# Keeping a recurrent state once for two heads and copying it out with GpSimd

## The chip, the cores and the metric

The kernel runs on one core of one Trainium2 chip. The metric is the device time of one execution in microseconds. A core has five engines that run side by side: TensorE (PE, matrix multiply, with its weight loads as PEld), VectorE (DVE), ScalarE (ACT), GpSimd (POOL) and SyncE (SP, here a queue of DMAs). They wait for each other through semaphores.

## The reference

Two blocks follow each other. The first is a gated linear recurrence for 4 batches of 8 heads, 768 tokens, head size 48: a 48 x 48 state a head is decayed row by row and given an outer product at each token, and a query reads it.

```python
f = 1.0 / (1.0 + np.exp(-f_logit))
for t in range(S):
    state = f[:, :, t, :, None] * state + einsum('bhd,bhe->bhde', k[:, :, t], v[:, :, t])
    y[:, :, t] = einsum('bhd,bhde->bhe', q[:, :, t], state)
```

The result is laid out as x, 3072 tokens by 384. The second block computes h = x @ w_in (384 to 2048), g = h * erf(softplus(h)), and g @ w_out (2048 to 384). Everything is float32.

## The kernel before, in words

The tokens are cut into 24 chunks g of 128 (six a batch), two chunks to a block of 256 tokens, and each chunk into two half chunks c of 64. Half chunks are numbered k = 2g + c. The eight heads are four pairs a; the head r of a pair lives on partitions 64r to 64r + 47. Each chunk passes these stages:

- `stage_d` (L381): a matmul with a triangle sums the logs of the decays (ps_d, L387), ACT takes exponentials (dp L390, kd L393), SP copies the decay totals of a chunk into `Tall` by DMA (L398, from chunk 3 on), VectorE makes the scaled q and k (qd L402, kd L406).
- `stage_t` (L410): TensorE transposes them (ps_t, L418); ACT or VectorE copies them out (qA L425, kT L427 or L429). Before that it runs a `late` state step of the chunk before, if there is one.
- `stage_s` (L450): TensorE computes the state increments dS (L467) and the scores (L475) into one PSUM tile `sc`; the scores are masked into qA, by VectorE (L503) or, in chunks 3 to 9, by ACT copies (L495) and GpSimd (L498). Then `next_state(2g)` runs at once and `next_state(2g + 1)` is put in `late`.
- `stage_y` (L511): 64 small matmuls (L532) read qA and `sv`; ACT copies the result to xT (L536).

`sv` is the operand buffer of L532, two of them in turn (`svs`). It holds for each head r and half chunk c the state on the partitions of that head, and the v rows on the other half of the partitions (loaded by DMA at L254, or by ACT at L251 in the first three chunks). y(g) reads the states that k = 2g - 1 and k = 2g left.

`next_state` (L433) works directly on `sv`: for each of the two heads it adds the increment from PSUM to the state in the old place and writes the new place (L445), and multiplies there by the totals (L446). The first half chunk of a batch has one multiply (L443), and GpSimd sets the state of that batch to zero (L455).

The second block hides in between: `hidden` (L594, evacuated by ACT at L601), `activate` (exp and tanh on ACT, L157, L160, L566; products on VectorE, L165, L568), `project_first` (L684) and `project` (L735, with sums by L622 and L743). In the first part of the run the weights are loaded as raw 64-bit words, and `round_piece` makes float32 of them: one ACT and six VectorE instructions a piece (L311 to L336), 16 pieces.

The order of all work is written out by hand: `slots` gives the sequence of TensorE's matmuls of an iteration, and the lists `at` and `todo` say at which slot a stage is called. Each engine takes its instructions in that order, and the framework adds the semaphore waits that data and buffers ask for. The `sc` tile comes from a pool with one buffer, and is taken anew in each `stage_s`.

Of the kernel before, what the change touches and what calls it, by code (L numbers as in the profile page):

```python
# [43 lines left out]
FP32 = mybir.dt.float32  # L44
# [30 lines left out]
def kernel(  # L75
# [33 lines left out]
    def fixed(name, shape, dtype=FP32, pool=const):  # L109
        return pool.tile(shape, dtype, name=name)  # L110
# [67 lines left out]
    ps_at = main.enter_context(tc.tile_pool(name="ps_at", bufs=2, space=PSUM))  # L178
    ps_moe = main.enter_context(tc.tile_pool(name="ps_moe", bufs=2, space=PSUM))

    NV, NQ, NG = 3, 3, 12
    ADJACENT = 5
    vts = [fixed(f"vt{i}", [P, d_model], pool=fix) for i in range(NV)]
# [6 lines left out]
    kds = [fixed(f"kd{i}", [P, H, DP], pool=fix) for i in range(2)]  # L190
    dps = [fixed(f"dp{i}", [P, H, DP], pool=fix) for i in range(2)]
    Tall = fixed("Tall", [P, n_chunks, 2, HP], pool=fix)
    Hring = fixed("Hg", [P, NG * FG * TB], pool=fix)

    DH = d_model // 2
# [237 lines left out]
    def next_state(k, dS):  # L433

        g, c = divmod(k, 2)
        g1, c1 = divmod(k + 1, 2)
        for r in range(2):
            old = svs[g % NSV][rows(r), r, c, :, PAD : PAD + D]
            new = svs[g1 % NSV][rows(r), r, c1, :, PAD : PAD + D]
            total = Tall[rows(r), g, c, :].unsqueeze(2).broadcast_to((D, HP, D))  # L440
            add = dS[rows(r), c, :].rearrange("p (a d) -> p a d", a=HP)
            if k % (2 * NCH) == 0:
                nc.vector.tensor_tensor(out=new, in0=add, in1=total, op=ALU.mult)  # L443
                continue
            nc.vector.tensor_tensor(out=new, in0=add, in1=old, op=ALU.add)  # L445
            nc.vector.tensor_tensor(  # L446
                out=new, in0=new, in1=total, op=ALU.mult
            )

    def stage_s(g):  # L450
        b, n = divmod(g, NCH)
        last = n == NCH - 1
        if n == 0:
            for r in range(2):
                nc.gpsimd.memset(svs[g % NSV][rows(r), r, 0, :, PAD : PAD + D], 0.0)  # L455
        qA, kT = qAs[g], kTs.pop(g)
        ps = ps_sc.tile([P, 2, 512], FP32, name="sc", tag="sc")

        sc = ps[:, :, 0 : HP * C].rearrange("s r (a t) -> s r a t", t=C)
        dS = ps[:, :, HP * C : HP * (C + D)]  # L460
        totals = ps[:, 0, HP * (C + D) : HP * (C + D) + 2 * HP]
        vt, kd = vts[g % NV], kds[g % 2]
        for a in range(HP):
            for c in range(1 if last else 2):
                for r in range(2):
                    h = 2 * a + r
                    nc.tensor.matmul(  # L467
                        dS[rows(r), c, D * a : D * (a + 1)],
                        lhsT=kd[half(c), h, 0:D], rhs=vt[half(c), D * h : D * (h + 1)],
                        start=True, stop=True,  # L470
                    )
        for a in range(HP):
            for r in range(2):
                for c in range(2):
                    nc.tensor.matmul(  # L475
                        sc[half(c), r, a, :], lhsT=kT[rows(r), a, half(c)],
                        rhs=qA[rows(r), r, a, half(c)], start=True, stop=True,
                    )
        if g < FIRST:

            pairs = dps[g % 2][:].rearrange("t (a r) d -> t a (r d)", r=2)
            for a in range(HP):
                nc.tensor.matmul(
                    totals[:, 2 * a : 2 * a + 2], lhsT=pairs[:, a, :], rhs=ident[:, C - 1 : P : C],
                    start=True, stop=True,
                )
            nc.vector.tensor_copy(
                out=Tall[:, g].rearrange("p c a -> p a c"),
                in_=totals.rearrange("p (a c) -> p a c", c=2),
            )  # L490
        for c in range(2):
            for r in range(2):
                if FIRST <= g < 2 * ADJACENT:

                    nc.scalar.copy(out=qA[half(1 - r), r, :, half(c)], in_=sc[half(c), r])  # L495
                    if c == 1:
                        flat = qA[half(1 - r), r].rearrange("s a (c t) -> s (a c) t", c=2)
                        nc.gpsimd.affine_select(  # L498
                            out=flat, in_=flat, pattern=[[0, 2 * HP], [1, C]], compare_op=ALU.is_ge,
                            fill=0.0, base=0, channel_multiplier=-1,  # L500
                        )
                    continue
                nc.vector.tensor_tensor(  # L503
                    out=qA[half(1 - r), r, :, half(c)], in0=sc[half(c), r],
                    in1=tri1[half(c)].unsqueeze(1).broadcast_to((C, HP, C)), op=ALU.mult,
                )
        next_state(2 * g, dS)
        if not last:
            late[g] = lambda: next_state(2 * g + 1, dS)
# [191 lines left out]
    def project(blk):  # L701


        ops = [ps_moe.tile([P, 2, 512], FP32, name="ops", tag="moe") for _ in range(2)]
        end = blk == n_blocks - 1
        ops.append(ps_sc.tile([P, 2, 512], FP32, name="ops", tag="sc") if end else ops[1])
        place = {n: ops[i][:, j, k * DH : (k + 1) * DH] for n, (i, j, k) in {
            1: (0, 0, 0), 2: (0, 1, 0), 6: (0, 1, 1), 5: (1, 0, 0), 7: (1, 0, 1), 3: (2, 1, 0), 4: (2, 1, 1),
        }.items()}
        first = [1, 2, 5, 3]  # L710
        if end:
            place[4] = ps_at.tile([P, 512], FP32, name="ops4", tag="at")[:, 0:DH]
            first.append(4)

        def pair(n):
            i, j = {2: (0, 1), 5: (1, 0), 3: (2, 1)}[n]
            return ops[i][:, j, 0 : 2 * DH].rearrange("p (n c) -> p n c", n=2)

        def products(gis, ns):
            for gi in gis:  # L720
                gr = groups[blk, gi]
                while gr["sums"] is None:
                    sum_step()
                a11, a12, a21, a22 = blocks(gr["h"])
                w = w_out_sb[:, FG * gi : FG * (gi + 1), :]
                s, t = gr["sums"], w_sums(gi)
                for j in range(2):
                    w1, w2 = w[:, j, :], w[:, 2 + j, :]
                    for n in ns:
                        x, y = {  # L730
                            1: (a11, w1[:, 0:DH]), 2: (a12, w2[:, 0:DH]), 3: (s[2], w2[:, DH:]),
                            4: (a22, t[:, 3, j, :]), 5: (s[0], t[:, 0, j, :]),
                            6: (s[1], t[:, 1, j, :]), 7: (a21, t[:, 2, j, :]),
                        }[n]
                        nc.tensor.matmul(  # L735
                            place[n], lhsT=x[:, j, :], rhs=y,
                            start=(gi == 0 and j == 0 and n in first),
                            stop=(gi == n_g - 1 and j == 1), skip_group_check=True,
                        )
                        yield  # L740

        def plus(out, x, y):
            nc.vector.tensor_tensor(out=out, in0=x, in1=y, op=ALU.add)  # L743

        o = rows_sb
        yield from products((0, 1), (1, 2, 6))
        yield from products((0,), (5, 7, 3, 4))
        to_sum.appendleft(sum_h(groups[blk, 3]))
        yield from products((1,), (5, 7, 3, 4))
        yield from products((2, 3), (1, 2, 6))  # L750
        nc.scalar.copy(out=o[:, 3, :], in_=place[1])  # L751

        plus(o[:, 0:5:4, :], o[:, 3:4, :].broadcast_to((P, 2, DH)), pair(2))
        def fives():

            plus(o[:, 3:5, :], o[:, 4:5, :].broadcast_to((P, 2, DH)), pair(5))

        yield from products((2, 3), (5, 7))
        if end:

            fives()
            yield from products((2, 3), (3,))
            plus(o[:, 1, :], o[:, 3, :], place[3])
            store_tile(blk, 0, nc.sync)
            plus(o[:, 3, :], o[:, 3, :], place[7])
            yield from products((2, 3), (4,))
            plus(o[:, 2, :], o[:, 4, :], place[4])
            store_tile(blk, 1, nc.scalar)
            return
        yield from products((2, 3), (3, 4))  # L770
        fives()
        plus(o[:, 1:3, :], o[:, 3:5, :], pair(3))
        plus(o[:, 3, :], o[:, 3, :], place[7])
        store(blk)
# [42 lines left out]
    with tc.manual_schedule():  # L817
# [62 lines left out]
        def weights_steps(n):  # L880
            for _ in range(n):
                weights_step()

        busy.append(ps_moe.tile([P, 2, 512], FP32, name="busy", tag="moe")[:, 0, 0:P])
        keep_busy(10)
        prepare(0, 0, 1)
# [340 lines left out]
```

## Time and profile before

| | |
|---|---|
| timed runs, median (3 runs) | 618.53 us (618.06 to 619.01) |
| span of the profiled execution | 616.6 us |
| that execution's own time beyond its span | not recorded; the median lies 1.9 us above the span |
| TensorE busy | 588.3 us (95%) |
| VectorE busy | 459.7 us (75%), 785 instructions |
| ACT busy | 382.9 us (62%) |
| GpSimd busy | 14.9 us (2%), 33 instructions |
| state instructions L443, L445, L446 | 8, 80 and 80, of 355, 354 and 358 ns |
| DMA engines, 0 to 16 us and 16 to 40 us | 98% and 96% busy |

The page gives each engine's busy time, rows of instructions grouped by line, and the chain of work that ended last: from the last instruction back, at each step to what released it. A row gives busy us, mean ns of one, and after the second bar the idle time of the engine just before, with what ended it. A timeline row gives start and length in us from the span's start. Time in which an engine idles but which lies beside a busy bottleneck costs nothing.

### The profile page before, as it was taken

How to read it: one execution, taken by the hardware profiler on the slowest of the kernel's cores; microseconds unless marked ns; L12 is line 12 of the kernel's file. 1: busy time of each engine (PE TensorE's matmuls, PEld its weight loads, DVE VectorE, ACT ScalarE, POOL GpSimd, SP SyncE). 2: the span in 40 equal slices, each digit the busy share in tenths (PEclk: the TensorE clock that was granted, in tenths of full speed). 3: DMA queues.
4: the chain of work that ended last, by engine and by line, in shares of the span. 5: the costliest groups of instructions: out<-in, count | busy, mean ns of one | idle time of the engine just before them, and what ended most of it. 6: DMA issues, size and time to landing. Idle time of an engine off the chain costs nothing.

```text
span 616.6 us, 13769 instructions
## 1 busy us (share of the span) xinstructions
PE 588.3 (95%) x5729; PEld 514.5 (83%) x5729; DVE 459.7 (75%) x785; ACT 382.9 (62%) x483; POOL 14.9 (2%) x33
## 2 busy tenths in 40 slices
PE   8778799999999999999999999999999999999996
PEld 7556688887655689989989988988988989989996
DVE  4898998697489597896896875896886795656651
ACT  5735365987875678875866585875775666366000
POOL 1000011010000000000000000000000000000000
PEclk9987899999999999999999999999999999999999
DMA  9998753441241222133133132042130000000000
GB/s 201 248 228 208 199 175 63 71 88 17 53 77 28 41 63 52 25 81 54 33 71 53 32 73 53 14 91 53 15 65 15 3 27 0 28 1 0 27 27 30
DMA packets 155604, 41.36 MB, mean 67 GB/s; under 512 B 147344, under 2 KB 150416, under 8 KB 155536
## 3 DMA queue, kind: packets, MB, share of 16 engines
q1 hardware_dynamic: 153312, 39.82, 29.6%
q8 instruction: 47, 0.77, 0.5%
q10 hardware_dynamic: 2224, 0.59, 0.4%
q14 instruction: 21, 0.17, 0.1%
HBM read 35.59 MB, written 4.72 MB: 65 GB/s over the span
## 4 chain that ended last, share of the span: by engine, by line
PE 74%; DVE 11%; ACT 8%; DMA 3%; issue 2%; SPq 1%; POOL 0%; DVEq 0%; ACTq 0%; POOLq 0%
PE hps L594 31%; PE ops L735 25%; PE ops L684 7%; PE y L532 3%; PE ps_t L418 3%; PE ps_d L387 2%; ACT x L160 2%; PE sc L467 1%; PE sc L475 1%; DVE sv L445 1%; DVE sv L446 1%; DVE w_in_sb L322 1%; DVE Hg L568 1%; DVE w_in_sb L336 1%; PE busy L379 1%
## 5 line engine op out<-in xcount | busy, mean ns | idle before, releaser
L594 PE MATMUL hps<-xT,w_in_sb 128*128 128x256 f32 x1152 | 264.7, 386 | 5.0 <-DVE w_in_sb L336 2.9
L594 PEld LDWEIGHTS hps<-xT,w_in_sb 128*128 128x128 f32 x1152 | 218.5, 193 | 39.2 <-ACT xT L536 2.8
L165 DVE SCALAR_TENSOR_TENSOR e<-x,e 128x1024 f32<-128x1024 f32 x96 | 117.1, 1220 | 13.2 <-ACT x L160 12.6
L160 ACT ACTIVATE x<-Hg,serf_bias 128x1024 f32<-128x1024 f32 x88 | 97.5, 1140 | 0.2
L157 ACT ACTIVATE e<-Hg 128x1024 f32<-128x1024 f32 x44 | 46.5, 1058 | 61.7 <-DVE Hg L568 57.6
L735 PE MATMUL ops<-wT,Hg 128*128 128x192 f32 x320 | 78.4, 328 | 0.0
L568 DVE TENSOR_TENSOR Hg<-Hg,e 128x1024 f32<-128x1024 f32 x44 | 53.7, 1222 | 22.6 <-ACT e L566 22.5
L735 PE MATMUL ops<-wT,scratch 128*128 128x192 f32 x288 | 67.8, 326 | 0.9 <-DVE scratch L743 0.9
L735 PE MATMUL ops<-w_out_sb,Hg 128*128 128x192 f32 x320 | 65.1, 326 | 0.0
L601 ACT COPY Hg<-hps 128x1024 f32<-128x1024 f32 x44 | 44.4, 1010 | 32.7 <-PE hps L594 32.4
L735 PEld LDWEIGHTS ops<-wT,Hg 128*128 128x128 f32 x320 | 55.7, 190 | 1.9
L735 PEld LDWEIGHTS ops<-w_out_sb,Hg 128*128 128x128 f32 x320 | 54.6, 190 | 2.0
L566 ACT ACTIVATE e<-e 128x1024 f32<-128x1024 f32 x48 | 50.3, 1048 | 1.9 <-DVE e L165 1.8
L735 PEld LDWEIGHTS ops<-wT,scratch 128*128 128x128 f32 x288 | 50.2, 190 | 1.1 <-issue 1.1
L503 DVE TENSOR_TENSOR qA<-sc,tri 64x256 f32<-64x256 f32 x68 | 28.7, 422 | 27.3 <-PE sc L475 26.3
L743 DVE TENSOR_TENSOR scratch<-scratch,ops 128x384 f32<-128x384 f32 (+1 forms) x41 | 20.3, 494 | 29.5 <-ACT scratch L751 23.0
L532 PEld LDWEIGHTS y<-qA,sv 128*32 128x32 f32 x1536 | 24.9, 113 | 19.6 <-issue 12.4
L532 PE MATMUL y<-qA,sv 128*32 128x64 f32 x1536 | 29.9, 226 | 10.9 <-issue 5.1
L425 ACT COPY qA<-ps_t 64x512 f32<-64x512 f32 x48 | 27.7, 577 | 19.4 <-PE ps_t L418 19.0
L402 DVE TENSOR_TENSOR qd<-qn,dp 128x384 f32<-128x384 f32 x24 | 13.4, 556 | 33.6 <-ACT dp L390 33.5
L735 PE MATMUL ops<-w_out_sb,scratch 128*128 128x192 f32 x144 | 34.7, 326 | 0.0
L445 DVE TENSOR_TENSOR sv<-sc,sv 48x192 f32<-48x192 f32 x80 | 28.3, 354 | 8.3 <-ACT qA L495 6.9
(111 smaller groups left out, 648.1 us busy)
## 6 DMA issues: line engine op xcount, KB each, us to landing
lt<-in_f_logit_dram SPq DMA_DIRECT2D x24, 192.0 KB, 3.7
qn<-in_q_dram SPq DMA_DIRECT2D x24, 192.0 KB, 3.4
kn<-in_k_dram SPq DMA_DIRECT2D x23, 192.0 KB, 3.7
vt<-in_v_dram SPq DMA_DIRECT2D x23, 192.0 KB, 3.7
out_dram<-scratch SPq DMA_DIRECT2D x11, 384.0 KB, 2.6
sv<-in_v_dram SPq DMA_DIRECT2D x84, 48.0 KB, 2.8
w_out_sb<-in_moe_w_in_dram SPq DMA_DIRECT2D x4, 768.0 KB, 6.1
Hg<-in_moe_w_in_dram SPq DMA_DIRECT2D x4, 768.0 KB, 6.6
```

Source lines behind the costliest of these rows:

```text
L157: nc.scalar.activation(out=dst[:], in_=h, func=AF.Exp)
L160: nc.scalar.activation(out=dst[:], in_=h, func=AF.Tanh, bias=serf_bias[:, i : i + 1], scale=SERF_KAB[i][0])
L165: nc.vector.scalar_tensor_tensor(out=e[:], in0=x[:], scalar=SERF_KAB[i][2], in1=e[:], op0=ALU.add, op1=ALU.mult)
L445: nc.vector.tensor_tensor(out=new, in0=add, in1=old, op=ALU.add)
L503: nc.vector.tensor_tensor(out=qA[half(1 - r), r, :, half(c)], in0=sc[half(c), r], in1=tri1[half(c)].unsqueeze(1).broadcast_to((C, HP, C)), ...
L532: nc.tensor.matmul(y[M * i : M * (i + 1), kt, half(c)], lhsT=sv[:, r, c, a, o : o + M], rhs=qA[:, r, a, half(c)], start=(n == 0), stop=Tru ...
L566: nc.scalar.activation(out=e[:], in_=e[:], func=AF.Tanh, scale=SERF_C)
L568: nc.vector.tensor_tensor(out=h, in0=h, in1=e[:], op=ALU.mult)
L594: nc.tensor.matmul(hps[:, j, :], lhsT=w_in_sb[:, kt, ft * P : (ft + 1) * P], rhs=xTs[blk][:, kt, :], start=(kt == 0), stop=(kt == n_k - 1),)
L601: nc.scalar.copy(out=gr["h"], in_=hps[:])
L684: nc.tensor.matmul(ops[:, tt, 0:d_model], lhsT=gr["h"][:, j, tt * P : (tt + 1) * P], rhs=w_out_sb[:, ft, :], start=(ft == 0), stop=(ft == ...
L735: nc.tensor.matmul(place[n], lhsT=x[:, j, :], rhs=y, start=(gi == 0 and j == 0 and n in first), stop=(gi == n_g - 1 and j == 1), skip_grou ...
```

## The change

The state of a pair's two heads is kept once, in a tile `state` of 128 partitions, of which rows 0 to 111 (48 of the one head, 16 unused, 48 of the other) are worked on by single instructions. A half chunk has one add (dS from PSUM plus `state`) and one multiply (by the totals), both in place, and then two GpSimd copies, one a head, from `state` into the new place in `sv`. The unused rows must hold numbers, so the PSUM tile `sc` is taken once for the whole run, and VectorE clears its increment part ahead of the first chunk. The last projection uses that tile where it took one from the pool.

```diff
+    sc_all = ps_sc.tile([P, 2, 512], FP32, name="sc", tag="sc")
...
+    STATE = DP + D
+    state = fixed("state", [P, HP, D], pool=fix)
...
         g, c = divmod(k, 2)
         g1, c1 = divmod(k + 1, 2)
+        total = Tall[0:STATE, g, c, :].unsqueeze(2).broadcast_to((STATE, HP, D))
+        add = dS[0:STATE, c, :].rearrange("p (a d) -> p a d", a=HP)
+        if k % (2 * NCH) == 0:
+            nc.vector.tensor_tensor(out=state[0:STATE], in0=add, in1=total, op=ALU.mult)
+        else:
+            nc.vector.tensor_tensor(out=state[0:STATE], in0=add, in1=state[0:STATE], op=ALU.add)
+            nc.vector.tensor_tensor(out=state[0:STATE], in0=state[0:STATE], in1=total, op=ALU.mult)
         for r in range(2):
-            old = svs[g % NSV][rows(r), r, c, :, PAD : PAD + D]
-            new = svs[g1 % NSV][rows(r), r, c1, :, PAD : PAD + D]
-            total = Tall[rows(r), g, c, :].unsqueeze(2).broadcast_to((D, HP, D))
-            add = dS[rows(r), c, :].rearrange("p (a d) -> p a d", a=HP)
-            if k % (2 * NCH) == 0:
-                nc.vector.tensor_tensor(out=new, in0=add, in1=total, op=ALU.mult)
-                continue
-            nc.vector.tensor_tensor(out=new, in0=add, in1=old, op=ALU.add)
-            nc.vector.tensor_tensor(
-                out=new, in0=new, in1=total, op=ALU.mult
+            nc.gpsimd.tensor_copy(
+                out=svs[g1 % NSV][rows(r), r, c1, :, PAD : PAD + D], in_=state[rows(r)]
             )
...
-        ps = ps_sc.tile([P, 2, 512], FP32, name="sc", tag="sc")
-
+        ps = sc_all
...
-        ops.append(ps_sc.tile([P, 2, 512], FP32, name="ops", tag="sc") if end else ops[1])
+        ops.append(sc_all if end else ops[1])
...
+        nc.vector.memset(sc_all[:, :, HP * C : HP * (C + D)], 0.0)
         busy.append(ps_moe.tile([P, 2, 512], FP32, name="busy", tag="moe")[:, 0, 0:P])
         keep_busy(10)
         prepare(0, 0, 1)
```

## The prediction

> **What bounds the kernel now.** I read the page's first part, then a table of busy time by stretch of the span, then the chain of work that ended last, and last the rows and the timeline of the concerned instructions.
>
> ```profile
> PE 588.3 (95%) x5729; PEld 514.5 (83%) x5729; DVE 459.7 (75%) x785; ACT 382.9 (62%) x483; POOL 14.9 (2%) x33
> ```
>
> TensorE is the bound as an average, but averages hide the stages. The table by stretch (window; then window length, busy us of each engine, granted clock, DMA share, GB/s) shows two:
>
> ```profile
> 16.00:72.00 56.00, 42.02 (x589) 33.45 (x587) 51.11 (x92) 27.28 (x49) 1.31 (x2) 0.88 0.90 235
> 72.00:130.00 58.00, 57.32 (x665) 48.19 (x666) 48.55 (x80) 42.44 (x66) 7.40 (x10) 0.97 0.47 102
> ...
> 220.00:500.00 280.00, 279.00 (x2935) 255.24 (x2934) 221.50 (x382) 195.96 (x228) 0.50 (x2) 1.00 0.24 45
> ```
>
> From 16 to 72 us TensorE is busy for 42.0 of 56 us and VectorE for 51.1. From 220 to 500 TensorE works 279 of 280 us, so no VectorE time saved there can move the end. Only the first stretch can. The chain confirms it (start, length, what):
>
> ```profile
> 24.67 0.36 DVE sv L445
> 25.05 0.35 DVE sv L446
> 25.43 0.37 DVE sv L445
> 25.83 0.36 DVE sv L446
> 26.21 0.97 DVE w_out_sb L331
> ...
> 71.65 0.48 DVE qd L402
> 72.12 0.14 issue
> 72.26 1.88 PE ps_t L418 x8
> ```
>
> From 17.5 us on the chain runs mostly over VectorE, until TensorE at 72.26 has waited 3.16 us for qd (L402) and takes over for good. The four state instructions of each half chunk lie on it, 0.385 us apart (24.67 to 26.21 is four). In this stretch VectorE idles only twice: 0.77 us for ACT at 17.49 (L313) and 1.85 us for ACT at 54.22 (L445).
>
> **What the Trainium skill says.** "SBUF — State Buffer", section "SBUF: two separate sides": VectorE and GpSimd share one port pair as an exclusive lock, held for a whole instruction; a VectorE instruction takes it in a 2-port mode or with two SBUF inputs, and the loser blocks. The trace agrees in part. Here GpSimd's masking of qA (L498) meets VectorE:
>
> ```profile
> 54.60 0.83 DVE L446 TENSOR_TENSOR sv<-sv,Tall 48x192 f32<-48x192 f32 x1
> ...
> 98.16 0.95 DVE L336 TENSOR_TENSOR w_out_sb<-w_out_sb 128x768 f32<-128x768 f32 x1
> ...
> 99.53 0.35 DVE L446 TENSOR_TENSOR sv<-sv,Tall 48x192 f32<-48x192 f32 x1
> 98.27 2.12 POOL L498 TENSOR_SCALAR_AFFINE_SELECT qA<-qA 64x512 f32<-64x512 f32 x2 [14.26 <-issue]
> ```
>
> L446, two SBUF inputs, usually 0.354, took 0.83 while L498 ran. The L498 pair that started during L336 took 2.12, where the undisturbed pair at 53.86 took 1.37: it was blocked some 0.75 us. But L446 at 99.53 also ran beside L498, undisturbed; there the two worked on different partitions (0 to 47 against 64 to 127), at 54.60 on the same. So I take the lock to bite where partitions overlap; nearly all VectorE work here is 128 partitions wide, so it will.
>
> "GPSIMD Engine Reference", section 4.1: an operation with one input runs at about line rate on GpSimd, one with two at half of VectorE's. The change gives GpSimd copies only. "VectorE: DVE Perf Modes", section "Rules for kernel authors": minimize the count of instructions. The trace agrees that partitions are free: 64x256 (L503) takes 422 ns, 128x256 (L622) 420 ns.
>
> **Part by part.** *VectorE instructions.* 44 half chunks: four begin a batch (one instruction a head), 40 have two a head.
>
> ```profile
> L446 DVE TENSOR_TENSOR sv<-sv,Tall 48x192 f32<-48x192 f32 x80 | 28.7, 358 | 2.8
> L445 DVE TENSOR_TENSOR sv<-sc,sv 48x192 f32<-48x192 f32 x80 | 28.3, 354 | 8.3 <-ACT qA L495 6.9
> ...
> L498 POOL TENSOR_SCALAR_AFFINE_SELECT qA<-qA 64x512 f32<-64x512 f32 x14 | 11.2, 803 | 157.6 <-issue 79.5 <-ACT qA L495 77.6
> ...
> L841 POOL COPY tri<-tri 64x64 f32<-64x64 f32 x2 | 0.5, 232 | 0.1
> ```
>
> 168 instructions become 84 of the same free size, so the same 0.355: 84 x 0.355 = 29.8 us off VectorE's 459.7. From 16 to 72 lie half chunks 0 to 7, where 1 + 7 x 2 = 15 go. At 0.385 that is 5.8; half chunk 0's share is worth nothing, as L313 behind it waits for ACT until 17.49 anyway. Left: 7 x 0.77 = 5.4 us. The other 69 go under a full TensorE: nothing. Their cover is TensorE's own work; if it went, each half chunk would be worth the same 0.77.
>
> *GpSimd copies*, 88 of 48x192. Price from both sides: above the 48x192 memset (L455, 0.252), below the 64x512 masking (0.651 to 0.701 undisturbed). Between the 64x64 copy (0.232) and that, by elements: 0.232 + 128 x 0.98 ns = 0.36. I take 0.35; ends 0.25 and 0.65. Two make 31 us on an engine with 14.9 of 616.6.
>
> *What the copies cost VectorE.* Right behind the multiply stands a wide instruction (L402, L331, L359, L313, L326: 0.35 to 0.96) that takes the lock before the multiply's completion reaches GpSimd. So a copy waits for it, then the next VectorE instruction waits for the copy. At 54.60 a 512-element masking cost VectorE 0.48; by elements a 192-element copy costs 0.18, at most its 0.35, at least 0 if the two slip past each other. I take 0.2: 14 copies, 2.8 us.
>
> *New waits.* The next add waits for both copies, since they read `state`. Where the adds stand close (half chunks 2 and 3: 2.0 us from the multiply's end to the next add) this can bind by some 0.3; it is within the 0.2 a copy. Queued behind that add is the whole rounding of weights. y(g) (L532) now waits for GpSimd in place of VectorE. From half chunk 8 on y stands over 3 us behind (state done 100.65, y at 104.07) or far more, and hides it. Earlier there are three tight hand-overs, y(1) at 26.24, y(2) at 38.31 and y(3) at 55.3: old completion was 1.5 us after the first add; new is add and multiply 0.73, a wait of 0 to 0.96, two copies 0.7, a wait between them: 1.5 to 3.2. So y(2) comes no earlier than before, and neither does ps_d(3) behind it; its dp from ACT ends at 41.82 + 0.49 = 42.31. qd (L402) at 43.43 can thus gain at most 1.1, though VectorE would have 5 x 0.77 - 10 x 0.2 = 1.85 by then. Lost: 0.75. At half chunk 6 the multiply covers both heads' partitions and still meets L498, as one of the two old ones did: no change. On GpSimd's queue the copies stand behind L498 of their own chunk, and the next L498 behind copies: it is over 10 us later. Copies wait for the y that last read the buffer, long done. SP's and ACT's queues keep their order.
>
> *PSUM tile kept once.* It removes the exchange of a tile whose readers were done; TensorE is shown to wait 0.2 us for L445 there in all. ACT's copies L495 get a wait for the previous add, done some 10 us before. Nothing.
>
> *Memset of the PSUM tile*, 384 elements, on VectorE ahead of the first clamp (L359, 4.31). 128 elements take 0.165 and 1280 take 1.125: 0.38. Behind it stand clamp, exp, ln (ending 5.74) and ps_d (6.08, behind warm-up matmuls). Some 0.2 is hidden; 0 to 0.4 is paid, I take 0.2.
>
> **Sum.** Until L402 of chunk 3: 1.1. Half chunks 6 and 7: 2 x 0.77 - 4 x 0.2 = 0.7. Memset: -0.2. Together 1.6 us earlier at 72.26, which TensorE can take, since it waits 3.16 there; from then on TensorE's work is the same. The profiled execution has a span of 616.6, and the median of the timed runs, 618.53, lies 1.9 above it. I forecast a span of 615.0 and 618.5 - 1.6 = 616.9. A result within 0.2% (1.24 us) of before can't be told from no change.
>
> **Rivals.**
> *The lock gives it back.* Copies hold VectorE for their full 0.35: 14 x 0.35 = 4.9 of 5.4, and the memset 0.2 against the 0.5 left: 618.2. For it: the skill's whole-instruction lock. Against: 0.48 at 54.60 was less than L498's 0.68.
> *The copies slip through.* The two heads lie on different partitions, and VectorE hardly stalls: then the gain is capped by TensorE's 3.16 us at 72.26: 618.5 - 3.2 + 0.2 = 615.5. For it: 99.53. Against: 54.60 and 98.27.
> *The hand-over to y becomes the bound (slower).* If each copy waits out a full 0.96 instruction, and copies cost nearer 0.65, both end 0.96 + 0.65 + 0.96 + 0.65 = 3.2 us behind the multiply, 1.7 later than a hand-over can bear even with 0.7 gained. Paid at y(2) and y(3), through ps_d and xT, twice 1.7 less 1.5 gained: 620.4. It decides once the second copy ends over about 2 us behind the multiply at y(1) to y(3). For it: L498 was blocked 0.75 once. Against: VectorE itself stays the later of the two at most places.
> *A 112-partition instruction costs more than a 48-partition one.* Against: 422 and 420 above. Then 618.7.
>
> **How the numbers follow.** Forecast 0.42 (own range 615.9 to 617.9), lock gives back 0.25, slips through 0.13, hand-over 0.17, wider instruction 0.03. Forecast counts as faster for about three quarters, slips through wholly: 0.45; hand-over is slower: 0.17; the rest 0.38. The range leaves out the outer part of the hand-over and the best of the slip: 615.0 to 620.0.
>
> **What would show it.** VectorE's busy time near 430 us; state instructions of 0.355 over 112 partitions; copies near 0.35, longer where a wide VectorE instruction started first; VectorE's L331, L336, L313 lengthened by about 0.2 behind them; ps_t of chunk 5 near 70.7 in place of 72.26; TensorE full after it. Wrong, if that ps_t is later than 72, if y(1) to y(3) wait for GpSimd over 1 us, or if time moves after 130 us.

## The result and the profile after

The changed kernel takes 613.04 us (median of 4 runs, 612.16 to 613.8) where the kernel before, run beside it on the same chip, takes 618.5; the ratio is 0.9914, with an interval of 0.99 to 0.9929. That is 5.5 us faster. The forecast was 616.9 with a range of 615.0 to 620.0: the direction was right, the size was not. The span of the profiled execution went from 616.6 to 610.9.

The page of the changed kernel, its busy line and the row of the new copies (two columns after the bar: busy us and mean ns; after the second bar the idle time before):

```profile
PE 588.6 (96%) x5729; PEld 514.6 (84%) x5729; DVE 428.7 (70%) x702; ACT 382.7 (63%) x483; POOL 92.8 (15%) x121
...
L449 POOL COPY sv<-state 48x192 f32<-48x192 f32 x88 | 76.3, 867 | 319.0 <-DVE state L447 222.9
```

VectorE lost 31.0 us, as forecast (29.8). A copy was to take 0.35. Its mean is 0.867, but the trace gives a minimum of 0.334, a median of 0.347 and a maximum of 3.99: the price alone was right, and some copies are held up for long.

The table by stretch, same columns as before:

```profile
16.00:72.00 56.00, 47.51 (x612) 38.30 (x611) 49.62 (x85) 30.36 (x54) 14.40 (x18) 0.85 0.91 238
72.00:130.00 58.00, 57.59 (x730) 48.22 (x729) 46.64 (x71) 43.83 (x68) 18.84 (x24) 1.00 0.47 99
...
220.00:500.00 280.00, 278.24 (x2925) 254.26 (x2924) 204.67 (x339) 193.37 (x225) 37.82 (x46) 1.00 0.23 45
```

From 16 to 72 us TensorE now works for 47.5 us instead of 42.0, on more matmuls (612 for 589) and at a lower granted clock (0.85 for 0.88). From 72 to 130 the granted clock is 1.00 where it was 0.97. And from 220 to 500 TensorE is busy for less than before, 278.2 instead of 279.0: something has begun to hold it there.

The chain of work around 25 us, where four state instructions stood before:

```profile
24.28 0.37 DVE state L446
24.65 0.02 issue
24.67 0.37 DVE state L447
25.04 0.05 issue
25.09 1.01 POOL sv L449
26.10 0.06 issue
26.16 0.97 POOL sv L449
27.13 0.04 issue
27.17 0.67 PE y L534 x28
```

VectorE and GpSimd over the same two microseconds (start, length):

```profile
24.28 0.36 DVE L446 TENSOR_TENSOR state<-sc,state 112x192 f32<-112x192 f32 x1
24.67 0.36 DVE L447 TENSOR_TENSOR state<-state,Tall 112x192 f32<-112x192 f32 x1
24.95 0.95 DVE L335 SCALAR_TENSOR_TENSOR w_out_sb<-w_out_sb 128x768 f32<-128x768 uint32 x1
25.94 0.97 DVE L340 TENSOR_TENSOR w_in_sb<-w_out_sb,w_in_sb 128x768 f32<-128x768 f32 x1
...
25.09 2.03 POOL L449 COPY sv<-state 48x192 f32<-48x192 f32 x2 [4.58 <-DVE state L447]
```

The two copies take 2.03 us instead of 0.7: each ends about 0.2 us after a wide VectorE instruction has ended (25.90, 26.91). L335 and L340 take 0.95 and 0.97, against 0.97 and 0.96 before. So at this place the one that yields is GpSimd, not VectorE. Also, L335 starts 0.28 us after the multiply; before, it started 0.38 after it (25.83 to 26.21). A half chunk thus saves 0.87 and not 0.77.

The late copies are on the chain, though. The second half of y(1) waited 0.71 us for them, and the chain goes on from it through ScalarE and TensorE, which ran at half clock from 27.95 to 38.19, to a wait of VectorE for TensorE's sums:

```profile
27.86 0.49 ACT xT L538
...
28.39 2.07 PE hps L596 x4
30.47 0.82 PE sc L469 x32
31.29 0.88 PE sc L477 x32
32.17 1.81 PE sc L485 x8
```

```profile
34.00 0.17 DVE L489 COPY Tall<-sc 128x8 f32<-128x8 f32 x1 [1.15 <-PE sc L485]
```

GpSimd's masking meets the multiply as it did before (the copies wait behind both):

```profile
52.15 0.77 DVE L447 TENSOR_TENSOR state<-state,Tall 112x192 f32<-112x192 f32 x1
...
51.35 1.37 POOL L500 TENSOR_SCALAR_AFFINE_SELECT qA<-qA 64x512 f32<-64x512 f32 x2 [7.29 <-ACT qA L497]
53.06 1.56 POOL L449 COPY sv<-state 48x192 f32<-48x192 f32 x2 [0.34 <-DVE state L447]
```

TensorE's take-over of the run, the transposes that waited 3.16 us at 72.26. (The prediction calls them chunk 5's. Counted from 0, as everywhere else, they are chunk 4's.)

```profile
68.09 0.63 PE L422 MATMUL ps_t<-ident,qd 128*128 128x128 f32 x4
68.56 0.63 PE L422 MATMUL ps_t<-ident,kd 128*128 128x128 f32 x4
```

They come 4.17 us earlier and wait for nothing. They are also shorter: 0.63 instead of 1.03 and 1.06, because TensorE ran at half clock there before and does not now. The twelve matmuls behind take 2.76 instead of 3.66. Near the end stands the loss. TensorE, then GpSimd and VectorE at the last y (chunk 23):

```profile
486.44 0.65 PE L534 MATMUL y<-qA,sv 128*32 128x64 f32 x32
488.70 1.04 PE L534 MATMUL y<-qA,sv 128*32 128x64 f32 x32 [1.61 <-POOL sv L449]
...
485.19 3.85 POOL L449 COPY sv<-state 48x192 f32<-48x192 f32 x2 [7.01 <-DVE state L447]
...
484.95 1.22 DVE L165 SCALAR_TENSOR_TENSOR e<-x,e 128x1024 f32<-128x1024 f32 x1
486.09 1.22 DVE L570 TENSOR_TENSOR Hg<-Hg,e 128x1024 f32<-128x1024 f32 x1
487.22 1.22 DVE L165 SCALAR_TENSOR_TENSOR e<-x,e 128x1024 f32<-128x1024 f32 x1
```

Behind three VectorE instructions in a row the two copies need 3.85 us, and the second half of y waits for them.

With the same instruction found in both traces, the lead of the changed kernel can be followed (start before, start after, lead):

| place | before | after | lead | what was added |
|---|---|---|---|---|
| transposes of chunk 4 | 72.26 | 68.09 | 4.17 | VectorE's shorter way |
| y(4) | 91.45 | 85.63 | 5.82 | +1.65, full clock behind the take-over |
| y(10) | 208.36 | 201.41 | 6.95 | +1.13, of it 1.04 at y(8) and y(9) |
| transposes of chunk 18 | 365.08 | 357.22 | 7.86 | +0.91, at one wait |
| end of the span | 616.6 | 610.9 | 5.7 | -2.2, the last y |

At y(8) and y(9) TensorE waited 1.37 and 1.51 us, and now 0.91 and 0.93. The profile names GpSimd for it, but its copies had ended at 144.90, and ACT's copy of qA ended at 145.44, 0.1 us ahead of y(8): y waits for ACT, which runs behind VectorE's L570. The one wait before chunk 18 was this line of before, which has no counterpart after:

```profile
361.12 4.12 PE L594 MATMUL hps<-xT,w_in_sb 128*128 128x256 f32 x18 [1.00 <-DVE scratch L743]
```

It is the one missing microsecond in "279 of 280". The table sets one profile beside one; over the profiles of all runs but one the first transposes start between 8.04 and 9.12 us (e7, below, is the exception).

### The profile page after: what moved, and what is told of

It is laid out like the page before. It is cut to its first block, busy times and chain, and to the rows that moved or that the text cites. A ratio compares the mean times of both kernels' runs of the same rounds, so it can differ in the third digit from the quotient of the medians.

```text
span 610.9 us, 13911 instructions
## 1 busy us (share of the span) xinstructions
PE 588.6 (96%) x5729; PEld 514.6 (84%) x5729; DVE 428.7 (70%) x702; ACT 382.7 (63%) x483; POOL 92.8 (15%) x121
## 3 DMA queue, kind: packets, MB, share of 16 engines
q1 hardware_dynamic: 153312, 39.82, 29.8%
## 4 chain that ended last, share of the span: by engine, by line
PE 81%; DVE 7%; ACT 7%; issue 2%; POOL 2%; ACTq 0%; POOLq 0%; DVEq 0%
PE hps L596 37%; PE ops L737 25%; PE ops L686 5%; PE y L534 3%; PE ps_t L422 3%; PE ps_d L391 2%; PE sc L477 2%; PE sc L469 2%; POOL sv L449 2%; ACT x L160 1%; DVE qA L505 1%; DVE Hg L570 1%; ACT e L568 1%; PE busy L383 1%; ACT e L157 1%
## 5 line engine op out<-in xcount | busy, mean ns | idle before, releaser
L449 POOL COPY sv<-state 48x192 f32<-48x192 f32 x88 | 76.3, 867 | 319.0 <-DVE state L447 222.9
L570 DVE TENSOR_TENSOR Hg<-Hg,e 128x1024 f32<-128x1024 f32 x44 | 53.7, 1221 | 24.6 <-ACT e L568 24.5
L737 PE MATMUL ops<-w_out_sb,scratch 128*128 128x192 f32 x132 | 32.2, 326 | 0.0
```

Of the source, the lines that this page charges most:

```text
L449: nc.gpsimd.tensor_copy(out=svs[g1 % NSV][rows(r), r, c1, :, PAD : PAD + D], in_=state[rows(r)])
L570: nc.vector.tensor_tensor(out=h, in0=h, in1=e[:], op=ALU.mult)
L737: nc.tensor.matmul(place[n], lhsT=x[:, j, :], rhs=y, start=(gi == 0 and j == 0 and n in first), stop=(gi == n_g - 1 and j == 1), skip_grou ...
```

## The experiments

Theory: what counts is VectorE's time before the take-over. It passes to TensorE in full, because GpSimd yields at the shared port. On top comes the half clock that no longer follows TensorE's wait, and the last y gives 2.2 us back. Rivals: the single PSUM tile; the steady part, where 69 of the 84 removed instructions lie; the lock at 0.2 us a copy; the clock coming at its own time.

### Which part of the run: e2, e3, and the tile alone: e1

e2 against the changed kernel; e3 has `>=` in place of `<`, and e1 is the kernel before with the lines of the change that concern `sc_all`:

```diff
     def next_state(k, dS):
...
+        if k < 2 * NCH:
+            total = Tall[0:STATE, g, c, :].unsqueeze(2).broadcast_to((STATE, HP, D))
...
+            return
+        for r in range(2):
+            old = svs[g % NSV][rows(r), r, c, :, PAD : PAD + D]
...
```

> The changed kernel, with the new state update for half chunks 0 to 10 alone (the first batch, to about 95 us), and the old one after that. Theory: the 4.2 us that reach TensorE's take-over and the 1.65 us of clock behind it are kept, together 5.8; the one or two later us that VectorE gained are lost, and so are the 2.2 us which the last y loses to GpSimd's copies: 612.7, between 612.2 and 613.4. Rival (the gain lies in the steady part, where most of the 84 removed instructions are): 616 or more.

> The reverse: the old state update in the first batch, the new one from half chunk 12 on (about 106 us). Theory: the wait of 3.16 us at TensorE's take-over and the half clock behind it are back; of the later changes some 2 us are gained and 2.2 lost at the last y: 618.3 to 619.2. Rival (gain in the steady part): 616 or less.

> The kernel before, with only two parts of the change: the PSUM tile is taken once, and its state columns are cleared at the start; the state is updated by four instructions as before. Theory (the gain is VectorE's shorter work in 16 to 72 us, and what follows from it): the clearing costs its 0.2 us and the tile is worth nothing, so 618.5 to 618.8. Rival (the exchange of the tile made TensorE or ScalarE wait, and keeping it is a good part of the 5.5 us): 617.5 or less.

| run | median us | before beside it | ratio (interval) |
|---|---|---|---|
| e2, new in the first batch | 611.92 | 618.15 | 0.9905 (0.9887 to 0.9924) |
| e3, new in the later batches | 620.53 | 618.15 | 1.0042 (1.0026 to 1.0057) |
| e1, tile and clearing alone | 618.37 | 618.15 | 1.0003 (0.9993 to 1.0013) |

All of the gain comes from 11 of the 44 half chunks (whether e2 is faster still than the changed kernel, the intervals leave open); e2 came out 0.3 below its expected range. The other 33 make the kernel slower. For e3 the expectation was too low by 1.3 us. Its trace has the wait at the last y, and there a clock loss that the trace of the changed kernel does not have (the row takes 1.47 where it took 1.04):

```profile
498.54 1.47 PE L548 MATMUL y<-qA,sv 128*32 128x64 f32 x32 [1.61 <-POOL sv L450]
```

With 1.65 us for one half-clock window that makes -0.95 and -0.95 (the same two gains in its trace), 2.26 for the wait, 1.65: +2.0 of the 2.4 measured; the rest stays open. (This profile alone also has a stop of 1.88 us at 234.76 that nothing in it explains; the other five timed executions of e3 are 3.4 to 5.6 us shorter.) The tile alone is worth nothing.

### Who yields at the shared port: e4, e7, e8, e11

e4 puts this behind the two copies of the changed kernel:

```diff
+        for r in range(2):
+            nc.gpsimd.tensor_copy(
+                out=spare[rows(r)], in_=ident[rows(r), 0:40].unsqueeze(1).broadcast_to((D, HP, 40))
+            )
```

e7 copies nothing (and clears the state part of `sv` once, on GpSimd, ahead of all):

```diff
-        for r in range(2):
+        for r in range(0):
             nc.gpsimd.tensor_copy(
```

e8, and in the same place e11 with `nc.scalar.copy(`:

```diff
-            nc.gpsimd.tensor_copy(
+            nc.vector.tensor_copy(
```

> The changed kernel with two more GpSimd copies behind the two real ones of every half chunk, each 160 elements of a constant on the same 48 partitions into a tile that nobody reads, so that only the shared port and GpSimd's queue feel them. Theory (GpSimd is the one that yields, VectorE loses some 0.02 us to a copy): VectorE's instructions behind the state update stay as long as they are (0.96 to 0.98 for the weight rounding), and the time is 613.0 to 613.8, the rest being real copies that queue behind extra ones. Rival (the prediction's: each copy costs VectorE 0.2 us): 14 extra copies before the take-over cost 2.8 us, so 615.8, and the instructions behind are longer by 0.2 each.

> The changed kernel without GpSimd's 88 copies: y reads operand buffers whose state part stays zero, so the carry from chunk to chunk is left out of y; all other work is done. It shows all that the copies cost. Theory (VectorE hardly notices them; they cost the wait at the last y, 2.2 us, and the short waits of two adds, 0.24 and less): 610.3 to 611.0, and VectorE's instructions behind the state update are as long as with copies. Rival (the prediction's lock, 0.2 us for each of the 14 copies before the take-over, 2.8 us, beside the last y): 608.5 or less.

> The changed kernel with the two copies of every half chunk on VectorE instead of GpSimd. A half chunk then has four VectorE instructions again, two of them without a second operand. Theory (the gain is VectorE time before the take-over, and GpSimd's copies are nearly free for VectorE): each copy costs VectorE 0.2 to 0.35, so of 0.87 us saved a half chunk 0.2 to 0.45 are left; TensorE's take-over comes 1 to 3 us earlier instead of 4.2; nothing waits at the last y: 614.0 to 617.0. Rival (what counts is only that the state is updated over both heads at once, not who copies): 613.1 or less.

> The changed kernel with ScalarE making the two copies of every half chunk instead of GpSimd. ScalarE copies of 64x256 (L497) take 0.37, so some 0.3 each, 27 us on an engine that is busy for 63% of the span. Theory (GpSimd is starved behind VectorE's back-to-back instructions, ScalarE isn't): each copy takes the same 0.3 or so wherever it stands, the last y waits less than 0.5 us, and the early stretch keeps its 4.2 us less what the copies delay of ScalarE's exponentials: 610.5 to 613.0. Rival (ScalarE's copies delay qA, exp and the activations more than GpSimd's starvation costs): 613.5 or more.

| run | median us | before beside it | ratio (interval) |
|---|---|---|---|
| e4, twice as many GpSimd copies | 613.09 | 618.15 | 0.9926 (0.9909 to 0.9942) |
| e7, none | 610.98 | 618.24 | 0.988 (0.9866 to 0.9895) |
| e8, copies on VectorE | 616.18 | 618.24 | 0.9966 (0.9954 to 0.9979) |
| e11, copies on ScalarE | 645.75 | 617.99 | 1.0434 (1.0409 to 1.0458) |

Doubling the copies costs nothing that the intervals show (the changed kernel had 0.9914). The same kind of row, after and in e4, shows VectorE all but untouched (before: 957 ns):

```profile
L340 DVE TENSOR_TENSOR w_in_sb<-w_out_sb,w_in_sb 128x768 f32<-128x768 f32 x4 | 3.8, 961 | 0.1
```

```profile
L341 DVE TENSOR_TENSOR w_in_sb<-w_out_sb,w_in_sb 128x768 f32<-128x768 f32 x4 | 3.8, 960 | 0.1
```

Matched one by one with the kernel before, VectorE's instructions from 16 to 72 us, those of the state left aside, grew by 0.43 us in all; by 0.67 with twice the copies, and by nothing without any (-0.05). Behind the take-over single ones grew by up to 0.45 (L340 at 92.78 took 1.40). So the lock as I priced it is refuted, and with it the rival in which it gives the gain back.

The total of e7 says less than it seems to. Its clearing on GpSimd holds VectorE up at the start (the first transposes come at 10.06), and behind its wait of 4.33 us at the take-over the half clock is back. Both work against what the missing copies save, and it is in part luck that the time falls within its expected range, near that of e6 below. Counted from the first transposes, qd of chunk 4 starts after 56.3 us in e7, and after 57.9 to 58.7 in the five profiles whose first batch has the copies (after, e2, e4, e6, e10). So the copies do cost the early stretch 1.6 to 2.3 us, mostly in waits: each of the five has the 0.24 for a copy and one wait of 1.2 to 1.4 that e7 lacks, for TensorE's L485 (after, e6, e10), for ScalarE's dp (e4) or for the DMA of the totals (e2). How much of that wait is the hand-over to y, and how much the half clock, which also lies elsewhere in e7, no run separates: in e2 y(1) waits the same 0.71 us for the copies, but at full clock behind it VectorE does not wait for L485.

In e8 the four VectorE instructions of a half chunk take 1.36 (23.89 to 25.25), against 1.54 before (24.67 to 26.21) and 0.67 after (24.28 to 24.95):

```profile
23.89 0.36 DVE L446 TENSOR_TENSOR state<-sc,state 112x192 f32<-112x192 f32 x1
24.29 0.36 DVE L447 TENSOR_TENSOR state<-state,Tall 112x192 f32<-112x192 f32 x1
24.68 0.54 DVE L449 COPY sv<-state 48x192 f32<-48x192 f32 x2
25.25 0.96 DVE L335 SCALAR_TENSOR_TENSOR w_out_sb<-w_out_sb 128x768 f32<-128x768 uint32 x1
```

qd of chunk 4 starts at 69.28, 2.3 us before the 71.56 of before, where the changed kernel has 4.2. (Seven times 0.18 makes 1.3 of it; 0.4 is there at the first transposes already, 8.44 instead of 8.83, no more than the starts of the profiles differ by; the rest I have not followed.) The 2.1 us measured are these 2.3: TensorE waits 5.34 us there, its transposes take 1.09, and the clock's part of the gain does not come. Joining the heads alone is thus worth about half of the early gain; moving the copies away brings the other half, and the clock.

In e11 the theory fell, by 33 us. A copy takes 0.35 on ScalarE as well, but ScalarE, too, takes its instructions in the order of the program. Its page and then its waits:

```profile
L449 ACT COPY sv<-state 48x192 f32<-48x192 f32 x88 | 30.8, 350 | 84.2 <-DVE state L447 76.1
```

```profile
ACT sv L449 <- DVE state L447: 76.1, 35, 5.8
```

At 35 places ScalarE stood for VectorE's multiply, 76.1 us in all and up to 5.8 at a time, with exponentials, qA and xT queued behind. I had priced the copies and forgotten their waits. GpSimd bears such waits too (222.9 us in the page's row above), at little cost: hardly anything but other copies is queued behind them.

### The clock behind TensorE's wait: e5, e9

e9 against the kernel before; e5 has `g == 5` and 20 matmuls:

```diff
     def stage_t(g):
...
+            if g == 4 and src is qd:
+                for _ in range(16):
+                    nc.tensor.matmul(ps[:, 0, :], lhsT=tri[:], rhs=tri[:], start=True, stop=True)
             for a in range(HP):
```

> The kernel before, with 20 matmuls of the constant triangle by itself put ahead of the transposes of chunk 5, where TensorE waits 3.16 us for qd; they write a PSUM region that the transposes then overwrite, and nobody reads them. At 0.14 us each (six took 0.83 at 16.02) they fill some 2.8 of the 3.16 us, so that TensorE is still ready when qd is. Theory (part of the gain came because the wait, and the half clock behind it, went): the 3.4 us behind the wait run at the full clock and everything after it comes 1.65 us earlier: 616.5 where the kernel before has 618.15. Rival (the half clock comes at its time whatever TensorE does, and all 5.5 us are VectorE's): no change, within 0.3 us.

> The kernel before, with 16 matmuls of the constant triangle by itself ahead of the transposes of chunk 4 (counted from 0), which is where TensorE really waits for qd at its take-over: the run that filled chunk 5 put them under a full TensorE. A profile showed 20 such matmuls to take 4.5 us at the full clock, so 16 take 3.6; the profiles of the old state update show waits of 3.16 to 5.6 us there, and the half clock in the 3.4 us behind in every one. They write a PSUM region that the transposes then overwrite. Theory (part of the gain came because the half clock behind the wait went): the transposes take 0.63 us instead of 1.03 to 1.09, and everything after comes 1.65 us earlier, less up to 0.45 where the fill outlasts the wait: 616.5 to 617.2 where the kernel before has 618.2. Rival (the half clock comes at its time whatever TensorE does): 618.1 or more.

e5 took 622.84 against 618.24 (ratio 1.008, 1.0067 to 1.0093). My slip with the chunk's number put the fill at 84.94, where TensorE had no wait; its 4.5 us came out as 4.6 us of time. It says nothing of the clock, but it measures that behind the take-over TensorE's work counts one to one. e9 took 616.62 against 617.99 (0.9981, 0.9972 to 0.999), 1.2 us less with an interval of 0.6 to 1.7. Its trace at the take-over:

```profile
66.40 3.73 PE L419 MATMUL ps_t<-tri 128*128 128x128 f32 x32
72.11 0.66 PE L421 MATMUL ps_t<-ident,qd 128*128 128x128 f32 x4 [1.97 <-DVE qd L402]
72.67 0.63 PE L421 MATMUL ps_t<-ident,kd 128*128 128x128 f32 x4
73.14 2.76 PE L597 MATMUL hps<-xT,w_in_sb 128*128 128x256 f32 x12
```

qd is no earlier than before (71.50), so VectorE gave nothing; y(4) starts at 89.75 instead of 91.45, 1.70 earlier: 0.15 of it is there at the transposes, the other 1.55 is the clock. Of 13 profiles (before, after, and eleven of the runs; e11's take-over lies elsewhere) these are the waits and the length of the four transposes behind:

| TensorE's wait at the take-over, us | runs | transposes, us |
|---|---|---|
| 5.60, 5.60, 5.34, 4.33, 3.94, 3.16 | e1, e3, e8, e7, e5, before | 1.03 to 1.09 |
| 2.41 | e12 | 0.63, half clock from about 1 us later |
| 1.97, 0.72, 0.65, 0.26, none, none | e9, e2, e4, e6, after, e10 | 0.63 to 0.66 |

The Trainium skill, "TensorE: Matmul & The Clock Gate", part 1, "The HAM clock gate", says that a free-running monitor halves TensorE's clock after an idle window of about 3.4 us. The traces agree on the length (each half clock lasts 3.41 us or twice or three times that, but for the last one, which the end of the run cuts); here a wait of 2.41 or 3.16, shorter than a window, was enough. Its length alone does not decide: the wait of 1.61 at the last y was followed by a half clock in e3 (498.95) and e4 (490.33), and not in the changed kernel.

### The last y: e6, e10

e6 against the changed kernel:

```diff
     def next_state(k, dS):
...
+        if k == 2 * (n_chunks - 1):
+            for r in range(2):
+                new = svs[g1 % NSV][rows(r), r, c1, :, PAD : PAD + D]
+                nc.vector.tensor_tensor(out=new, in0=add[rows(r)], in1=state[rows(r)], op=ALU.add)
+                nc.vector.tensor_tensor(out=new, in0=new, in1=total[rows(r)], op=ALU.mult)
+            return
```

e10 has besides:

```diff
-        nc.vector.memset(sc_all[:, :, HP * C : HP * (C + D)], 0.0)
         busy.append(ps_moe.tile([P, 2, 512], FP32, name="busy", tag="moe")[:, 0, 0:P])
         keep_busy(10)
         prepare(0, 0, 1)
+        nc.vector.memset(sc_all[:, :, HP * C : HP * (C + D)], 0.0)
```

> The changed kernel, but in the last half chunk (46) VectorE adds and multiplies from the kept state straight into the operand buffers, one add and one multiply a head, with no GpSimd copy. Theory: the last y, whose second half waited 1.61 us for the starved copies, runs through, and 2.2 us (488.70 less 486.44) come back: 610.9, between 610.3 and 611.5. Rival (VectorE's four instructions, or the sums behind them, bind there instead, or the end is set elsewhere): 612.5 or more.

> The changed kernel with the last half chunk written directly by VectorE, and with the clearing of the PSUM tile's state columns moved behind the first clamp, where VectorE is idle for 3 us. Theory: the 0.19 us by which the clearing delays the first clamp, and with it VectorE's whole early stretch, comes back on top of the last y: 0.2 below the kernel with the last half chunk alone (610.3), so 610.1, between 609.5 and 610.7. Rival (the 0.2 us are hidden behind TensorE's warm-up or ScalarE): 610.3; the two are closer than this measurement tells apart, and it is run as the best version.

e6 took 610.32 against 618.24 (0.9875, 0.9861 to 0.989), e10 610.0 against 617.99 (0.9874, 0.9852 to 0.9896). In e6 the last y runs in one go:

```profile
486.17 1.10 PE L540 MATMUL y<-qA,sv 128*32 128x64 f32 x64
```

One half chunk of 44, given back to VectorE, is worth some 2.5 us (7.9 below the kernel before beside it, against 5.5). Both beat the changed kernel. What the later clearing adds in e10 can't be told from nothing.

### The order of the heads: e12

Against the kernel before:

```diff
     def next_state(k, dS):
...
-        for r in range(2):
+        for r in (1, 0):
```

> The kernel before, with the second head of each pair (partitions 64 to 111) updated ahead of the first (0 to 47). Everything else is as before. Theory (an instruction that starts at another partition quarter than the last one is held about 0.1 us longer, which is why a half chunk saved 0.87 instead of 0.77): the instruction behind the last multiply now starts 0.28 us after it instead of 0.38, while the first add starts 0.1 later, behind an instruction that begins at partition 0; the sum and the time are unchanged, 618.2. Rival (the 0.1 us has to do with the single PSUM tile, the kept state or the number of partitions): the instruction behind the last multiply still starts 0.38 us after it.

It took 615.36 against 617.99 (0.9962, 0.9949 to 0.9974): 2.4 us faster, with a line that I had expected to change nothing. The last multiply and what follows it, in e12:

```profile
25.59 0.35 DVE L446 TENSOR_TENSOR sv<-sv,Tall 48x192 f32<-48x192 f32 x1
25.86 0.95 DVE L331 SCALAR_TENSOR_TENSOR w_out_sb<-w_out_sb 128x768 f32<-128x768 uint32 x1
```

The spacing is 0.28 (0.27 as printed), so the 0.1 us has to do with the partition at which the instruction ahead begins, and not with the kept state or the number of partitions. That much the theory said. Its other half was wrong: the first add does not start later (18.65 against 18.66). The Trainium skill, "VectorE: DVE Perf Modes", section "Two Vector instructions with no wait between them", says that an instruction is held until all earlier ones have finished if its operands start in another quarter of the partitions than the last ones. In both orders the first add starts 0.01 us or more behind the end of the instruction ahead: it has no early start to lose; the wide instruction has. The changed kernel, in which every state instruction begins at partition 0, gains there too: at three of the seven half chunks that count (18.75, 39.35, 57.99) the add starts 0.08 to 0.09 ahead of that end. At the take-over qd starts at 70.49 instead of 71.56, and TensorE's wait falls from 3.16 to 2.41. The lead in the trace grows from 1.0 at y(4) to 1.5 at y(9) and 1.85 at the last y; the timed 2.4 (1.6 to 3.2) is at the edge of that. The profiled execution, 616.64 at a mean clock of 0.984, is one of the slower of the ten; six lie between 615.1 and 615.4, at 0.988 to 0.991, so they had less half clock than the trace shows. Where, and why each step of the later part is gained, I have not followed.

## Why the prediction was off, point by point

**The bound and the place: right.** VectorE from 16 to 72 us, TensorE behind it. e2 shows it, and e5 that TensorE's time counts one to one after the take-over.

**84 x 0.355 off VectorE: right** (31.0). A 112-partition instruction takes 354 and, undisturbed, 357 ns. That rival is out.

**0.77 a half chunk: too small.** It is 0.87, by the held instruction (e12), and another 0.1 at the three first adds named there. Seven half chunks: 1.0 us.

**Copies cost VectorE 0.2 each, 2.8 us: the step that failed.** Up to the take-over VectorE's wide instructions grew by 0.01 to 0.02, at two places by 0.14, 0.43 us in all; one add waited 0.24 for the copies; e4's doubled copies cost no time that shows. What else they cost there is no lock: it is part of VectorE's 1.15 us at 34.00, behind a TensorE that y(1) had held up. From the collision at 54.60 I took that the lock bites where partitions overlap, and that both sides pay. The multiply at 99.53, which I read as undisturbed on other partitions, overlaps the masking ahead of it, which ends at 99.63, by 0.10 us only; the next one (99.69) begins behind it, and on its own partitions. e12 refutes the first: there the multiply of partitions 64 to 111 takes 0.83 at 53.79, while GpSimd masks partitions 0 to 63. As to who pays, VectorE runs with few gaps and is mostly there first. The line at 98.27, GpSimd blocked for 0.75 beside an unharmed L336, stood in the prediction and said so. The Trainium skill, "SBUF — State Buffer", section "SBUF: two separate sides", gives the shared ports to whoever starts first, for the whole instruction; that VectorE's own L447 is held where GpSimd came first (0.77 at 52.15), and the copies nearly everywhere else, agrees with it.

**qd of chunk 3 can gain at most 1.1: failed.** It came 2.55 earlier (43.43 to 40.88). I held y(2) and ACT's dp to their old times. But y(2), which had waited 1.02 and 0.47 for VectorE, ran in one go and ended 0.46 earlier, and ps_d behind it took 0.81 instead of 1.46, at full clock; so dp stood ready at 40.71 instead of 42.31. A time that another engine owes to the one being shortened is no cap.

**An add that waits some 0.3 for the copies at half chunks 2 and 3: right** (0.24 at half chunk 3). **Clearing 0.2: not shown.** The changed kernel's first qd is 0.19 later than before (8.32, 8.13), but with the same clearing e1 has 7.99 and e6 7.77. **The old collision unchanged: right** (0.77 at 52.15).

**The sum, 1.6, for 4.17.** In its place: seven half chunks at 0.87 and 0.3 for the three adds make 6.4. Off it go 0.19 at the start, 0.24 for dp of chunk 1, 0.24 for the copies, 0.43 for longer instructions, and 1.15 at 34.00. That leaves 4.15, where 4.17 were measured.

**"TensorE's work is the same from then on": failed.** It is the same work but not the same clock: 1.65 us in the trace of the changed kernel, 1.55 in e9's.

**Slack of 3.16 as a cap on the gain (rival "slips through"):** its mechanism was the right one, its cap was not. TensorE's own way to 72 us also ran over VectorE, through the rounded weights: its waits for L336 fell from 2.9 to 0.5 us. Nor was 3.16 a property of the kernel: e1 and e3, with the old state update in this stretch, waited 5.60, since TensorE had come there at 66.5 and 66.8 instead of 69.1, with its half clock in other windows.

**"No VectorE time saved from 220 to 500 can move the end": wrong by one wait.** 279 of 280 left one us for VectorE's L743, and that one was gained. Between 130 and 220, TensorE had idle time that I did not look at; 1.13 were gained there.

**Hand-over to y, the slower rival: right in kind, wrong in size and place.** I looked for it at y(1) to y(3), where the longest case of the sum is 3.35 (0.73, 0.96, 0.7 and 0.96), not 3.2. At y(1) it is part of the 1.15 above. The large one came at y(23), at 488.70, for 2.2 us: this y follows its own scores (481.72) after 4.7 us, where from 220 to 480 it is some 22. I had covered everything from half chunk 8 on with "over 3 us behind"; the trace of before has the last L446 ending at 493.64 and y(23) starting at 494.30, 0.66 behind. In e3, without the early gain, this wait and the half clock behind it make the kernel slower.

## What to carry over

Before pricing a contention, ask who is queued without gaps: in these runs that engine nearly always won the port, and the other one's work comes late by the length of what stands in its way, so the question becomes who waits for the loser. Work that has to wait for another engine belongs on an engine with nothing behind it in its queue, and a copy there is nearly free until somebody needs it at once. When a wait of the bottleneck engine goes, look at its clock behind that wait as well, and when a stretch is "full", look up what the last per cent waits for.

## What the runs showed of the hardware

- A GpSimd copy of 48x192 took 0.334 at the least and 0.347 in the median, a pair 0.74 at its quickest; behind three 1024-element VectorE instructions a pair took 3.85, and behind seven instructions of 384 to 1024 elements in a row a single copy took 3.99. ScalarE takes 0.350, VectorE 0.274 (mean of 88).
- VectorE beside these copies: 0.961 for a 128x768 instruction, against 0.957 without; all its other instructions from 16 to 72 us, beside 16 copies, 0.43 longer together.
- A VectorE instruction with nothing to wait for starts 0.28 behind the start of a 0.36 us one that begins at partition 0, and 0.38 behind one that begins at partition 64. Swapping two heads, so that the last one begins at partition 0, was worth 2.4 us.
- A TensorE wait of 2.41 us or more at the take-over was followed by half clock in 7 of 7 profiles, one of 1.97 or less in 0 of 6; elsewhere 1.61 was followed by one in two profiles and not in a third. One window of 3.41 us cost 1.55 to 1.65.
